# Four scalings of w_out moved from ScalarE to GpSimd, with a new hand-written order of steps

## The chip, the cores and the metric

The kernel runs on one core of a Trainium2 chip. The core has five engines that work side by side, each through its own queue in order: TensorE (PE in the profile; its weight loads are shown as PEld), VectorE (DVE), ScalarE (ACT), GpSimd (POOL) and SyncE (SP, which here only issues transfers). The metric is the device time of one execution in microseconds (us). Before the change it is 273.89 us, the median of three runs (273.89 to 274.06).

## What is computed

Two layers follow one another. The first is an attention without softmax, whose features are products of two small sketches; the second is a wide layer with a rational activation, applied to the first one's result.

```python
# attention: q, k, v are 4 batches x 4 heads x 1088 positions x 32; S1, S2 are 8 x 32
def phi(x):
    a = np.einsum('rd,bhsd->bhsr', S1, x)
    b = np.einsum('rd,bhsd->bhsr', S2, x)
    return np.einsum('bhsi,bhsj->bhsij', a, b).reshape(*x.shape[:-1], r * r)
q_p, k_p = (phi(q), phi(k))
kv = np.einsum('bhsf,bhsd->bhfd', k_p, v)
z = np.sum(k_p, axis=2)
num = np.einsum('bhsf,bhfd->bhsd', q_p, kv)
den = np.einsum('bhsf,bhf->bhs', q_p, z)[..., None] + 1e-06
x = num / den                        # then reshaped to 4352 tokens x 128
# wide layer: w_in is 128 x 2048, w_out is 2048 x 128
h = x @ w_in
P = a[0] + a[1] * h + a[2] * h2 + a[3] * h3
Q = 1.0 + np.abs(b[0]) * np.abs(h) + np.abs(b[1]) * h2
out = (P / (Q + 1e-06)) @ w_out
```

Here h2 and h3 are the square and the cube of h.

## The kernel before

**How the work is cut.** The tokens of the wide layer are cut into pieces, and with the 2048 hidden columns they make 17 units, numbered 0 to 16, of 128 x 4096 hidden values each. Unit 0 has the first 256 tokens and all its hidden columns, units 1 to 14 have 512 tokens and half the columns, units 15 and 16 have 256 tokens again. A unit's hidden values are made in four parts of 1024 columns and worked on in two halves of 2048.

**A unit's steps.** `hidden` (step h, line 448) is the matmul of tokens with w_in into a pair of PSUM tiles; `evac` (e, line 454) is ScalarE's copy of it to bf16, named hh; `d_abs`, `d_w`, `d_y` (u, w, y; lines 477, 483, 488, VectorE) make the denominator; `a_ln` and `a_exp` (ln, ex; lines 539, 543, ScalarE) turn it into its reciprocal r; the linear factor p = a3 h + a2 (pa on ScalarE, line 534, or pd on VectorE, line 529; the table `P_ON_ACT` says which, for each half of a unit); `d_s`, `d_hs`, `d_g` (s, m, x; lines 547, 551, 562, VectorE) multiply hh, r and p. In the halves listed in `HORNER` the factors are taken in another order, with one more small step (v, line 557). `gather` (G, line 581) is the output matmul of r, s and g with three scaled copies of w_out, so that P is never formed: the copy for r is a0 w_out, the one for s is a1 w_out, and the one for g is w_out in bf16. `store` (st, line 590) transposes an output tile on VectorE and writes it.

**The scaled copies of w_out.** `fetch_w` (step lw, line 643) loads w_out in two halves of 512 KB into a buffer, `w_out_sb_f`, that shares two slots with the w tiles of the units. `w_part` (step wo, lines 610 to 618) makes the three bf16 copies, each in two halves of 128 x 1024: wo:0 and wo:1 times a0, wo:2 and wo:3 times a1, wo:4 and wo:5 plain. The table `W_ENG` gives the engine of each: four on ScalarE and two (wo:2 and wo:4) on VectorE.

**The attention.** `Keys` has the steps kt, ks, kc, kf, kp, kk: VectorE transposes k, TensorE makes the sketches, ScalarE copies one of them, VectorE multiplies them to features, TensorE multiplies these with v, and ScalarE keeps the sums (`kvz`). Batch 0 does this in three parts, so as to begin early. `Queries` has qt, qs, qc, qf, qp (the same for q, then the numerators and denominators), qd, qi, qx (denominator, reciprocal, quotient), qb (a transpose on TensorE) and qk (ScalarE's copy into `xT`, what `hidden` reads). Batch 0 has four blocks, 0 to 3; the later batches have three each. From block 3 on, the sketches go through DRAM to be spread over the partitions (`Spread`, lines 395 to 426).

**What sets the order.** Nothing is scheduled by a planner at run time. `ORDER`, lines 21 to 57, is a list of 726 steps written as name:number; the program issues them in that order, so each engine's queue holds its share of them in the same order, and semaphores make a step wait for what it reads and for the buffers that it reuses. A step that isn't ready holds up everything behind it on its engine. The steps lx, lk, lv, lq, lw are loads on SP's queue; tn issues idle matmuls (line 170), as many as `TURNS` says: tn:0 ten, tn:1 and tn:4 two each.

Of the kernel before, what the change touches and what calls it, by code (L numbers as in the profile page):

```python
# [20 lines left out]
ORDER = """
tn:4 tn:0 lw:1 kt0:0 lq:0 kt2:0 lw:0 kt3:0 lx:1 kt1:0 ks0:0 lk:1 qt:0 ks2:0 kc0:0 lx:0 kf0:0 ba:0 qt:1 tn:1 kc2:0 qs:0
kf2:0 kp0:0 qc:0 ks1:0 qf:0 kc1:0 kf1:0 qs:1 wo:1 qt:3 kp1:0 qc:1 kp2:0 qf:1 qt:2 qs:3 wo:4 kk:0 lq:1 lv:1 wo:2 qp:0
wo:0 qs:2 qd:0 wo:5 qi:0 qx:0 qc:2 qb:0 qf:2 qk:0 wo:3 qp:1 kt0:1 qc:3 h2:0 qd:1 qi:1 qx:1 qt:5 h3:0 e2:0 qt:4 kt1:1
qp:2 e3:0 h1:0 pa1:0 u1:0 w1:0 h0:0 y1:0 qd:2 e1:0 qi:2 qx:2 qs:4 e0:0 qb:1 qb:2 qt:6 ks1:1 qk:1 u0:0 qk:2 ln1:0 w0:0
ks0:1 y0:0 h1:1 lk:2 kc1:1 ex1:0 lq:2 kf1:1 h3:1 e1:1 s1:0 kc0:1 h0:1 e3:1 kf0:1 pa0:0 m1:0 h2:1 qf:3 e0:1 x1:0 qp:3
qc:4 e2:1 kt0:2 h0:2 ln0:0 u1:1 kt1:2 h1:2 w1:1 e0:2 ex0:0 y1:1 ks0:2 h2:2 e1:2 s0:0 qd:3 ln0:1 h3:2 qi:3 m0:0 e2:2
lk:3 qx:3 kp1:1 x0:0 e3:2 ex0:1 u1:2 qb:3 lv:2 G0:0 pd0:1 qk:3 w1:2 ln1:1 G1:0 G2:0 qf:4 G3:0 kc0:2 kk:1 y1:2 ex1:1
G4:0 G5:0 kf0:2 qp:4 ln0:2 s0:1 qs:5 G0:1 qd:4 qc:5 qi:4 ex0:2 qt:7 G1:1 qx:4 m0:1 qb:4 ks1:2 qk:4 s1:1 pa1:1 h2:3
s0:2 kc1:2 m1:1 h3:3 e2:3 kf1:2 h1:3 e3:3 st:0 x1:1 ln1:2 qs:7 x0:1 h0:3 e1:3 kt1:3 m0:2 h2:4 e0:3 pd1:2 pa0:2 u1:3  # L30
h3:4 qt:9 w1:3 e2:4 G2:1 ex1:2 x0:2 h0:4 qf:5 e3:4 kp1:2 s1:2 pa0:3 y1:3 h1:4 qc:7 e0:4 m1:2 ln0:3 qp:5 kt0:3 e1:4
G3:1 x1:2 ex0:3 G4:1 m0:3 G5:1 u1:4 ks0:3 qd:5 ln1:3 qi:5 G0:2 w1:4 G1:2 pa1:3 qx:5 G2:2 y1:4 lv:3 qb:5 G3:2 qk:5
ex1:3 h0:5 m1:3 v0:3 kk:2 ln0:4 h2:5 s1:3 e0:5 qs:6 G4:2 qf:7 ex0:4 h1:5 x0:3 qt:8 qc:6 e2:5 s0:4 e1:5 h3:5 pd0:4
pa1:4 m0:4 h1:6 v1:3 e3:5 x0:4 G5:2 ln1:4 u1:5 h3:6 st:2 e1:6 w1:5 qp:7 ex1:4 x1:3 h0:6 e3:6 y1:5 qd:7 pa0:5 lq:3 G0:3
G2:3 qi:7 s1:4 h2:6 e0:6 m0:5 ln0:5 m1:4 qs:8 G3:3 e2:6 qf:6 G5:3 x1:4 ex0:5 G0:4 u1:6 G1:4 qc:8 ln1:5 qp:6 v0:5 qx:7
w1:6 qb:7 qd:6 G2:4 pa0:6 qi:6 G3:4 qx:6 y1:6 qb:6 qk:7 G4:4 qk:6 ex1:5 h3:7 m0:6 pa1:5 G5:4 qt:10 s1:5 h1:7 e3:7 st:4
h2:7 e1:7 m1:5 ln0:6 x0:5 h0:7 e2:7 x1:5 qs:9 e0:7 h3:8 qf:8 ex0:6 u1:7 h1:8 v0:6 qc:9 ln1:6 w1:7 ks1:3 s0:6 e1:8 G0:5
y1:7 kc1:3 qp:8 ex1:6 h2:8 pd1:6 kc0:3 e3:8 s1:6 ln0:7 h0:8 kf0:3 e2:8 m1:6 G2:5 ex0:7 G3:5 x0:6 G4:5 kf1:3 qd:8 e0:8
qs:10 G5:5 ln1:7 qi:8 u1:8 kp1:3 qx:8 pa0:7 w1:8 qb:8 G0:6 qf:9 qk:8 y1:8 qc:10 h3:9 ex1:7 s0:7 h2:9 e3:9 s1:7 ln0:8
h0:9 m0:7 e2:9 x1:6 G2:6 e0:9 h1:10 x0:7 ex0:8 pd1:7 h1:9 m1:7 pa0:8 s0:8 G3:6 e1:9 u1:9 G0:7 qt:11 ln1:8 qp:9 qt:12  # L40
u0:9 m0:8 h3:10 e1:10 w1:9 qd:9 ex1:8 qf:10 h2:10 x0:8 e3:10 G4:6 x1:7 e2:10 h0:10 y1:9 kk:3 pa0:9 w0:9 qp:10 qi:9
y0:9 e0:10 G1:7 qx:9 qd:10 ln0:9 s1:8 qb:9 G5:6 qi:10 u1:10 G2:7 qk:9 ex0:9 G3:7 qx:10 m1:8 qb:10 G4:7 qk:10 ln1:9
pd1:8 h1:11 s0:9 w1:10 ex1:9 qs:11 h0:11 m0:9 e1:11 x1:8 G5:7 qc:11 e0:11 h3:11 y1:10 pa1:9 h2:11 s1:9 e3:11 ln0:10
x0:9 G0:8 h0:12 m1:9 e2:11 pd0:10 ex0:10 h1:12 u1:11 x1:9 G1:8 ln1:10 w1:11 G0:9 G2:8 e1:12 s0:10 G3:8 e0:12 y1:11
h2:12 ex1:10 G4:8 m0:10 ln0:11 G1:9 qf:11 G5:8 s1:10 ex0:11 h3:12 x0:10 pa1:10 m1:10 qs:12 G2:9 s0:11 G3:9 e2:12 G4:9
pd0:11 qc:12 ln1:11 m0:11 qp:11 x1:10 G5:9 e3:12 x0:11 G0:10 qd:11 ex1:11 G1:10 qi:11 u1:12 G2:10 pa1:11 qx:11 G3:10
w1:12 qb:11 G4:10 s1:11 qk:11 pa0:12 h1:13 y1:12 h2:13 e1:13 m1:11 ln0:12 h3:13 st:6 x1:11 ex0:12 G5:10 qf:12 st:10
qp:12 e2:13 s0:12 e3:13 h0:13 st:8 ln1:12 m0:12 h2:14 u1:13 e0:13 x0:12 ex1:12 h3:14 u0:13 w1:13 e2:14 w0:13 G0:11
s1:12 e3:14 h1:14 pa1:12 y0:13 h0:14 m1:12 qd:12 e1:14 y1:13 G1:11 e0:14 qi:12 pd0:13 G2:11 ln1:13 qx:12 G3:11 u1:14
G4:11 ex1:13 x1:12 G5:11 w1:14 qb:12 G0:12 qk:12 ln0:13 G1:12 s1:13 h0:15 y1:14 ex0:13 h2:15 m1:13 e0:15 ln0:14 s0:13  # L50
h1:15 pd1:13 e2:15 m0:13 ex0:14 h3:15 x1:13 x0:13 e1:15 G2:12 e3:15 s0:14 G3:12 pa0:14 G4:12 u1:15 h2:16 m0:14 ln1:14
w1:15 G5:12 h3:16 x0:14 ex1:14 y1:15 G0:13 e2:16 G1:13 e3:16 s1:14 h0:16 ln0:15 st:12 u3:16 G2:13 u2:16 e0:16 w3:16
h1:16 w2:16 ex0:15 y3:16 pd0:15 G3:13 y2:16 e1:16 s0:15 G4:13 pa1:14 G5:13 u0:16 m0:15 G0:15 ln1:15 G1:15 w0:16 m1:14
G0:14 G1:14 ex1:15 y0:16 G2:14 pd1:15 G3:14 ln0:16 v1:14 x0:15 s1:15 ex0:16 G2:15 G3:15 x1:14 G4:15 ln2:16 m1:15 G0:16
ex2:16 s0:16 pa0:16 x1:15 G1:16 G5:14 s2:16 pa3:16 m0:16 G5:15 ln3:16 m2:16 x0:16 ex3:16 st:14 pa2:16 G2:16 s3:16
G3:16 st:15 G4:16 x2:16 m3:16 G5:16 G6:16 x3:16 G7:16 G8:16 st:16
""".split()
# [12 lines left out]
def kernel(  # L70
# [128 lines left out]
    for i in range(2):  # L199
        nc.vector.tensor_mul(out=S12[:, :, i, :],  # L200
                             in0=sT[i][:, None, 0:R].broadcast_to([128, H, R]),
# [408 lines left out]
    def w_part(x):  # L610
        y, f = x // 2, x % 2 * (nf // 2)
        o, t = w_sb[y][:, f:f + nf // 2], w_out_sb_f[:, f:f + nf // 2]
        if y == 2:
            (nc.scalar.copy if W_ENG[x] else nc.vector.tensor_copy)(out=o, in_=t)
        elif W_ENG[x]:
            nc.scalar.activation(out=o, in_=t, func=ACT.Copy, scale=a_sb[:, y:y + 1])
# [94 lines left out]
```

## Time and profile before

| | |
|---|---|
| median of three runs | 273.89 us (273.89 to 274.06) |
| the profiled execution | 274.08 us, of which its span, first to last instruction, 272.3 us |
| TensorE, busy | 258.4 us, 95% of the span |
| VectorE, busy | 256.0 us, 94% |
| ScalarE, busy | 250.2 us, 92% |
| GpSimd, busy | 2.9 us, 1%, all before 4.8 us |
| last VectorE instruction ends | 268.4 us; what follows is the last store |

Three engines are nearly full, so a share of the whole span does not tell them apart. The profile can be asked for a stretch of the span instead, for the instructions of a line, for a timeline of single instructions with the wait ahead of each in brackets, and for the waits of all engines added up. A line of the timeline gives the start, the length, the engine, the line of the kernel, the operation, and output <- inputs with their shapes; x12 at its end means that twelve in a row were drawn together.

### The profile page before, as it was taken

What the parts mean: (1) busy time and instruction counts of PE and PEld (TensorE: products, weight loads), DVE (VectorE), ACT (ScalarE), POOL (GpSimd) and SP (SyncE); (2) the same over time, 40 slices, a digit from 0 to 9 for tenths busy, and PEclk for the clock granted to TensorE, in tenths of its full rate; (3) what the DMA queues carried; (4) which work ended last, traced back from release to release, by engine and by line L of the source; (5) the groups of instructions that cost most, each with busy time, mean ns of one, the idle gap of its engine ahead of it and who ended that gap; (6) DMA issues with size and microseconds to landing.
All of it is one profiled execution on the core that took longest, in us unless ns stands there. A gap on an engine that the chain in (4) does not pass through costs nothing.

```text
span 272.3 us, 3730 instructions
## 1 busy us (share of the span) xinstructions
PE 258.4 (95%) x1398; PEld 146.2 (54%) x1398; DVE 256.0 (94%) x277; ACT 250.2 (92%) x224; POOL 2.9 (1%) x24
## 2 busy tenths in 40 slices
...
GB/s 166 290 330 99 196 14 183 101 50 100 2 80 135 12 136 81 67 78 39 96 6 115 12 0 4 40 90 0 14 97 90 25 0 0 2 24 14 1 7 74
DMA packets 30530, 19.55 MB, mean 72 GB/s; under 512 B 20400, under 2 KB 26672, under 8 KB 30512
## 3 DMA queue, kind: packets, MB, share of 16 engines
...
q8 instruction: 11, 0.18, 0.3%
...
## 4 chain that ended last, share of the span: by engine, by line
PE 35%; ACT 28%; DVE 23%; issue 9%; DMA 2%; SPq 1%; DVEq 0%; ACTq 0%
PE h_ps L448 17%; PE att_ps L581 9%; ACT hh L454 8%; ACT ln L539 7%; ACT r L543 7%; DVE s L547 4%; ACT p L534 4%; DVE g L551 4%; PE att_ps L361 3%; DVE g L562 3%; DVE w L488 3%; DVE w L483 2%; DMA k_sb<-in_k_dram 2%; PE att_ps L298 1%; PE att_ps L257 1%
## 5 line engine op out<-in xcount | busy, mean ns | idle before, releaser
L448 PE MATMUL h_ps<-xT,w_in_sb 128*128 128x512 f32 (+1 forms) x320 | 126.2, 536 | 2.3 <-ACT hh L454 1.6
L448 PEld LDWEIGHTS h_ps<-xT,w_in_sb 128*128 128x128 f32 x320 | 58.3, 190 | 52.8 <-issue 35.0
L454 ACT CAST hh<-h_ps 128x1024 bf16<-128x1024 f32 x68 | 68.2, 1022 | 4.2 <-PE h_ps L448 3.7
L581 PEld LDWEIGHTS <-w_out 128*128 128x128 bf16 x460 | 44.6, 98 | 46.0 <-issue 15.1
L543 ACT ACTIVATE r<-ln 128x2048 bf16<-128x2048 f32 (+1 forms) x35 | 65.9, 1883 | 0.3
L539 ACT ACTIVATE ln<-w 128x2048 f32<-128x2048 bf16 (+1 forms) x35 | 65.9, 1882 | 0.3
L534 ACT ACTIVATE p<-hh,a_sb 128x2048 bf16<-128x2048 bf16 (+1 forms) x23 | 46.7, 2035 | 0.1
L547 DVE TENSOR_TENSOR s<-hh,r 128x2048 bf16<-128x2048 bf16 (+2 forms) x33 | 40.9, 1243 | 0.2
L488 DVE TENSOR_TENSOR w<-w,u 128x4096 bf16<-128x4096 bf16 (+2 forms) x22 | 39.5, 1798 | 0.1
L581 PE MATMUL att_ps<-g,w_out 128*128 128x512 bf16 (+1 forms) x160 | 34.8, 347 | 3.6 <-DVE g L562 3.6
L551 DVE TENSOR_TENSOR g<-hh,s 128x2048 bf16<-128x2048 bf16 (+1 forms) x30 | 35.2, 1175 | 0.0
L581 PE MATMUL att_ps<-r,w_out 128*128 128x512 bf16 (+1 forms) x160 | 35.0, 347 | 0.0
L562 DVE TENSOR_TENSOR g<-g,p 128x2048 bf16<-128x2048 bf16 (+1 forms) x30 | 34.9, 1175 | 0.0
L581 PE MATMUL att_ps<-s,w_out 128*128 128x512 bf16 (+1 forms) x140 | 29.8, 343 | 0.9 <-DVE s L547 0.9
L483 DVE TENSOR_SCALAR w<-u,b_abs 128x4096 bf16<-128x4096 bf16 (+2 forms) x22 | 23.9, 1092 | 0.1
L477 DVE TENSOR_SCALAR u<-hh 128x4096 uint16<-128x4096 uint16 (+2 forms) x22 | 21.2, 968 | 0.9 <-ACT hh L454 0.8
L361 PEld LDWEIGHTS att_ps<-kvz,q_pT 128*128 128x128 f32 x144 | 17.6, 191 | 4.9 <-ACT sk_sb L408 1.0
L361 PE MATMUL att_ps<-kvz,q_pT 128*128 128x66 f32 x144 | 18.0, 274 | 0.9 <-DVE q_pT L353 0.5
L298 PEld LDWEIGHTS att_ps<-v_sb,k_p 128*64 128x64 f32 (+1 forms) x288 | 8.8, 138 | 2.6 <-issue 1.8
L529 DVE TENSOR_SCALAR p<-hh,a_sb 128x2048 bf16<-128x2048 bf16 x12 | 9.6, 799 | 0.0
L298 PE MATMUL att_ps<-v_sb,k_p 128*64 128x64 f32 (+1 forms) x288 | 9.5, 224 | 0.0
L425 DVE TENSOR_TENSOR q_pT<-a_all,b_all 128x768 f32<-128x768 f32 (+1 forms) x10 | 9.0, 896 | 0.0
...
## 6 DMA issues: line engine op xcount, KB each, us to landing
...
```

Source lines behind the costliest of these rows:

```text
L361: nc.tensor.matmul(self.nd[:, o:o + 2 * KW], lhsT=self.q_p[:, c, x:x + 128], rhs=kvz[self.b % 2][:, c, :], start=True, stop=True)
L448: nc.tensor.matmul(t[:, x * tl:(x + 1) * tl], lhsT=w_in_sb[:, f * 128:(f + 1) * 128], rhs=xT[:, t0:t0 + tl], start=True, stop=True)
L454: nc.scalar.copy(out=live[i]["hh"][:, part * PW:(part + 1) * PW], in_=live[i]["h", part])
L483: nc.vector.tensor_scalar(out=t[:, c], in0=live[i]["u"][:, c], scalar1=ab1, scalar2=ab0, op0=AX.mult, op1=AX.add)
L488: nc.vector.tensor_mul(out=t[:, c], in0=t[:, c], in1=live[i]["u"][:, c])
L534: nc.scalar.activation(out=part_of(i, "p", h), in_=hh, func=ACT.Identity, scale=a3, bias=a2)
L539: nc.scalar.activation(out=t, in_=live[i]["w"][:, span(h)], func=ACT.Ln, bias=1.0 + 1e-6)
L543: nc.scalar.activation(out=part_of(i, "r", h), in_=live[i]["ln"], func=ACT.Exp, scale=-1.0)
L547: nc.vector.tensor_mul(out=part_of(i, "s", h), in0=hh, in1=part_of(i, "r", h))
L551: nc.vector.tensor_mul(out=part_of(i, "g", h), in0=hh, in1=part_of(i, "p" if horner(i, first(h)) else "s", h))
L562: nc.vector.tensor_mul(out=g, in0=g, in1=part_of(i, "s" if horner(i, first(h)) else "p", h))
L581: nc.tensor.matmul(outs[t0][:, :tl], lhsT=w_sb[y][:, f0 + x, :], rhs=part_of(i, key, h)[:, c:c + tl], start=done[0] == 0, stop=done[0] == ...
```

## The change

`W_ENG` names GpSimd (2) for the four parts that ScalarE made, `w_part` learns that value, and `ORDER` is a new arrangement of the same 726 steps. `P_ON_ACT` and `HORNER`, which settle the engine and the form of each linear factor, are as they were, and so are `TURNS` and the lists of wide steps.

```diff
-W_ENG = (1, 1, 0, 1, 0, 1)
+W_ENG = (2, 2, 0, 2, 0, 2)
 P_ON_ACT = (1, 1, 0, 1, 1, 0, 1, 1, 0, 1, 1, 1, 1, 0, 1, 0, 1, 0, 1, 1, 0, 1, 0, 1, 1, 1, 0, 0, 1, 1, 0, 0, 1, 1)
...
         y, f = x // 2, x % 2 * (nf // 2)
         o, t = w_sb[y][:, f:f + nf // 2], w_out_sb_f[:, f:f + nf // 2]
         if y == 2:
-            (nc.scalar.copy if W_ENG[x] else nc.vector.tensor_copy)(out=o, in_=t)
+            (nc.vector.tensor_copy, nc.scalar.copy, nc.gpsimd.tensor_copy)[W_ENG[x]](out=o, in_=t)
+        elif W_ENG[x] == 2:
+            nc.gpsimd.tensor_scalar(out=o, in0=t, scalar1=a_sb[:, y:y + 1], scalar2=None, op0=AX.mult)
         elif W_ENG[x]:
             nc.scalar.activation(out=o, in_=t, func=ACT.Copy, scale=a_sb[:, y:y + 1])
```

The beginning of `ORDER`, up to the first steps on the second half of unit 0:

```diff
-tn:4 tn:0 lw:1 kt0:0 lq:0 kt2:0 lw:0 kt3:0 lx:1 kt1:0 ks0:0 lk:1 qt:0 ks2:0 kc0:0 lx:0 kf0:0 ba:0 qt:1 tn:1 kc2:0 qs:0
-kf2:0 kp0:0 qc:0 ks1:0 qf:0 kc1:0 kf1:0 qs:1 wo:1 qt:3 kp1:0 qc:1 kp2:0 qf:1 qt:2 qs:3 wo:4 kk:0 lq:1 lv:1 wo:2 qp:0
-wo:0 qs:2 qd:0 wo:5 qi:0 qx:0 qc:2 qb:0 qf:2 qk:0 wo:3 qp:1 kt0:1 qc:3 h2:0 qd:1 qi:1 qx:1 qt:5 h3:0 e2:0 qt:4 kt1:1
-qp:2 e3:0 h1:0 pa1:0 u1:0 w1:0 h0:0 y1:0 qd:2 e1:0 qi:2 qx:2 qs:4 e0:0 qb:1 qb:2 qt:6 ks1:1 qk:1 u0:0 qk:2 ln1:0 w0:0
...
+tn:0 lq:0 kt0:0 lx:1 kt2:0 lx:0 ks0:0 lw:0 kt3:0 kt1:0 ks2:0 kc0:0 lk:1 kf0:0 lw:1 qt:1 ks1:0 kc2:0 ba:0 tn:1 kf2:0
+kc1:0 tn:4 kp0:0 qt:0 qs:0 kf1:0 kp1:0 qt:2 qc:0 kp2:0 qf:0 qs:2 kk:0 lv:1 qc:2 qp:0 qs:1 qd:0 qf:2 qt:3 qp:2 wo:0
+qc:1 qi:0 lq:1 qx:0 qf:1 qs:3 qd:2 qb:0 qi:2 wo:4 qp:1 qk:0 qc:3 h3:0 qd:1 qi:1 qx:1 wo:2 wo:3 qx:2 h2:0 e3:0 kt0:1
+wo:1 kt1:1 h0:0 e2:0 wo:5 pa1:0 u1:0 h1:0 w1:0 y1:0 e0:0 ks1:1 qt:5 e1:0 qt:4 qb:2 qb:1 qs:4 qk:2 u0:0 qk:1 ln1:0 h1:1
+qt:6 w0:0 y0:0 kc1:1 ex1:0 h3:1 kf1:1 lk:2 ks0:1 e1:1 s1:0 lq:2 kc0:1 h0:1 e3:1 kf0:1 pa0:0 m1:0 h2:1 qf:3 x1:0 qc:4
...
```

In both kernels qd is a VectorE instruction for blocks 0 and 1 and a ScalarE instruction for all others.

More of the change, by code (lines that the diff above doesn't have):

```diff
@@ L21 @@
 ORDER = """
-tn:4 tn:0 lw:1 kt0:0 lq:0 kt2:0 lw:0 kt3:0 lx:1 kt1:0 ks0:0 lk:1 qt:0 ks2:0 kc0:0 lx:0 kf0:0 ba:0 qt:1 tn:1 kc2:0 qs:0
-kf2:0 kp0:0 qc:0 ks1:0 qf:0 kc1:0 kf1:0 qs:1 wo:1 qt:3 kp1:0 qc:1 kp2:0 qf:1 qt:2 qs:3 wo:4 kk:0 lq:1 lv:1 wo:2 qp:0
-wo:0 qs:2 qd:0 wo:5 qi:0 qx:0 qc:2 qb:0 qf:2 qk:0 wo:3 qp:1 kt0:1 qc:3 h2:0 qd:1 qi:1 qx:1 qt:5 h3:0 e2:0 qt:4 kt1:1
-qp:2 e3:0 h1:0 pa1:0 u1:0 w1:0 h0:0 y1:0 qd:2 e1:0 qi:2 qx:2 qs:4 e0:0 qb:1 qb:2 qt:6 ks1:1 qk:1 u0:0 qk:2 ln1:0 w0:0
-ks0:1 y0:0 h1:1 lk:2 kc1:1 ex1:0 lq:2 kf1:1 h3:1 e1:1 s1:0 kc0:1 h0:1 e3:1 kf0:1 pa0:0 m1:0 h2:1 qf:3 e0:1 x1:0 qp:3
@@ L27 @@
[L27 to L56, printed above, removed]
+tn:0 lq:0 kt0:0 lx:1 kt2:0 lx:0 ks0:0 lw:0 kt3:0 kt1:0 ks2:0 kc0:0 lk:1 kf0:0 lw:1 qt:1 ks1:0 kc2:0 ba:0 tn:1 kf2:0
@@ new lines @@
+kc1:0 tn:4 kp0:0 qt:0 qs:0 kf1:0 kp1:0 qt:2 qc:0 kp2:0 qf:0 qs:2 kk:0 lv:1 qc:2 qp:0 qs:1 qd:0 qf:2 qt:3 qp:2 wo:0
+qc:1 qi:0 lq:1 qx:0 qf:1 qs:3 qd:2 qb:0 qi:2 wo:4 qp:1 qk:0 qc:3 h3:0 qd:1 qi:1 qx:1 wo:2 wo:3 qx:2 h2:0 e3:0 kt0:1
+wo:1 kt1:1 h0:0 e2:0 wo:5 pa1:0 u1:0 h1:0 w1:0 y1:0 e0:0 ks1:1 qt:5 e1:0 qt:4 qb:2 qb:1 qs:4 qk:2 u0:0 qk:1 ln1:0 h1:1
+qt:6 w0:0 y0:0 kc1:1 ex1:0 h3:1 kf1:1 lk:2 ks0:1 e1:1 s1:0 lq:2 kc0:1 h0:1 e3:1 kf0:1 pa0:0 m1:0 h2:1 qf:3 x1:0 qc:4
+e0:1 qp:3 e2:1 kt0:2 h0:2 ln0:0 u1:1 h1:2 w1:1 qd:3 e0:2 ex0:0 kt1:2 y1:1 ks0:2 h2:2 e1:2 s0:0 ln1:1 h3:2 qi:3 m0:0
@@ new lines @@
+e2:2 kp1:1 qx:3 e3:2 x0:0 ex1:1 u1:2 qb:3 lv:2 G0:0 w1:2 qk:3 ln0:1 G1:0 y1:2 lk:3 G2:0 G3:0 kc0:2 ex0:1 qs:5 qf:4
+G4:0 kk:1 kf0:2 qc:5 qp:4 pa1:1 s0:1 G5:0 qt:7 qd:4 ln0:2 G0:1 qi:4 pd0:1 G1:1 qx:4 s1:1 qb:4 qs:7 qk:4 ex0:2 m0:1
+h3:3 m1:1 ln1:2 h2:3 s0:2 x0:1 ks1:2 e3:3 m0:2 e2:3 h0:3 kc1:2 pa0:2 st:0 kf1:2 h1:3 x1:1 e0:3 qs:6 e1:3 x0:2 h3:4
+ex1:2 u1:3 h0:4 pd1:2 e3:4 w1:3 pa0:3 h2:4 qf:5 y1:3 qp:5 qc:7 e0:4 e2:4 h1:4 s1:2 ln0:3 qt:9 kp1:2 m1:2 e1:4 kt0:3
+qd:5 ex0:3 x1:2 G2:1 G3:1 kt1:3 pa1:3 u1:4 G4:1 qi:5 G5:1 w1:4 lv:3 ln1:3 G0:2 qx:5 G1:2 qt:8 y1:4 lq:3 ex1:3 qb:5
@@ new lines @@
+G2:2 G3:2 qk:5 m1:3 G4:2 ln0:4 G5:2 qf:7 h1:5 s1:3 kk:2 qc:6 ex0:4 h0:5 m0:3 e1:5 ln1:4 v1:3 h2:5 s0:4 e0:5 v0:3 qp:7
+pd0:4 e2:5 m0:4 h3:5 ex1:4 x1:3 h3:6 qd:7 e3:5 x0:4 pa1:4 u1:5 h1:6 s1:4 e3:6 ks0:3 w1:5 e1:6 h0:6 pa0:5 st:2 x0:3
+h2:6 y1:5 e0:6 qs:8 e2:6 G0:3 m1:4 ln0:5 G2:3 G3:3 qf:6 qi:7 G5:3 m0:5 qc:8 ex0:5 qp:6 x1:4 G0:4 u1:6 qd:6 ln1:5 G1:4
+qi:6 w1:6 G2:4 pa0:6 G3:4 qx:7 qx:6 qb:7 y1:6 qb:6 qk:7 G4:4 qk:6 ex1:5 h1:7 m0:6 ln0:6 h3:7 s1:5 G5:4 e1:7 v0:5 e3:7
+h2:7 v0:6 kc0:3 pa1:5 m1:5 h0:7 qt:11 qf:8 e2:7 x1:5 qp:8 e0:7 kf0:3 ex0:6 qs:9 h3:8 u1:7 qc:9 ln1:6 x0:5 h1:8 w1:7
@@ new lines @@
+ex1:6 ks1:3 s0:6 G0:5 y1:7 kc1:3 e1:8 G2:5 qd:8 e3:8 G3:5 kf1:3 G4:5 ln1:7 h0:8 pd1:6 ex1:7 s1:6 h2:8 x0:6 e0:8 qi:8
+G5:5 m1:6 e2:8 G0:6 qx:8 ln0:7 u1:8 qb:8 kp1:3 qt:10 qk:8 w1:8 pa0:7 h2:9 qf:9 y1:8 ex0:7 qs:10 h3:9 qc:10 e2:9 x1:6
+ln0:8 qp:9 st:4 s0:7 h0:9 e3:9 pd1:7 ex0:8 m0:7 h1:9 s1:7 e0:9 x0:7 G2:6 kk:3 qd:9 e1:9 G3:6 s0:8 pa0:8 h1:10 u0:9
+m1:7 ln1:8 h3:10 u1:9 w0:9 e1:10 m0:8 G0:7 e3:10 G4:6 w1:9 ex1:8 h2:10 x0:8 y1:9 pa0:9 h0:10 y0:9 qi:9 G5:6 qf:10
+e0:10 x1:7 qp:10 ln0:9 qt:12 G1:7 qx:9 s1:8 qd:10 e2:10 qb:9 G2:7 qk:9 qi:10 u1:10 ex0:9 G3:7 G4:7 qx:10 m1:8 ln1:9
```

14 lines of the change are left out of this document (added).

## The prediction

> **What bounds the kernel now.** I read the busy times by stage first, because the page's single share (VectorE 94%, ScalarE 92%, TensorE 95%) averages over a start, a long middle and an end. The columns are the stretch, its length, then busy us and instructions of PE, PEld, DVE, ACT and POOL, the clock, and DMA share and GB/s.
>
> ```profile
> 6.00:28.00 22.00, 20.56 (x190) 16.59 (x189) 16.73 (x34) 14.12 (x25) 0.00 (x0) 1.00 0.84 241
> 28.00:266.50 238.50, 231.63 (x1190) 127.02 (x1190) 237.23 (x237) 234.78 (x199) 0.00 (x0) 1.00 0.22 54
> 266.50:272.30 5.80, 1.37 (x13) 0.96 (x10) 1.14 (x2) 0.00 (x0) 0.00 (x0) 0.95 0.45 66
> ```
>
> From 28.0 to 266.5 us VectorE is busy 237.23 of 238.50: it stands still 1.27 us in all. So in the middle the end is set by how much VectorE work is left at 28 us. Before that it is idle 5.3 of 22 us and TensorE is the fullest. The waits that remain are short (total us, times, longest):
>
> ```profile
> DVE qT L321 <- DMA q_sb<-in_q_dram: 2.1, 1, 2.1
> DVE out_sb L590 <- PE att_ps L581: 1.0, 2, 0.7
> DVE u L477 <- ACT hh L454: 0.8, 3, 0.3
> ```
>
> Only the first is large, and it lies in the start. There I read the timeline (start, length, engine, line, operation):
>
> ```profile
> 11.50 1.15 ACT L616 ACTIVATE w_out<-w_out_sb_f,a_sb 128x1024 bf16<-128x1024 f32 x1
> ...
> 14.93 1.15 ACT L616 ACTIVATE w_out<-w_out_sb_f,a_sb 128x1024 bf16<-128x1024 f32 x1
> ...
> 15.98 1.03 ACT L614 CAST w_out<-w_out_sb_f 128x1024 bf16<-128x1024 f32 x1
> ...
> 17.87 1.17 ACT L616 ACTIVATE w_out<-w_out_sb_f,a_sb 128x1024 bf16<-128x1024 f32 x1
> ...
> 17.96 1.11 PE L361 MATMUL att_ps<-kvz,q_pT 128*128 128x66 f32 x8 [0.52 <-DVE q_pT L353]
> ...
> 18.90 3.67 PE L448 MATMUL h_ps<-xT,w_in_sb 128*128 128x256 f32 x16
> ...
> 20.88 1.01 ACT L454 CAST hh<-h_ps 128x1024 bf16<-128x1024 f32 x1 [1.66 <-PE h_ps L448]
> ...
> 23.65 0.69 DVE L477 TENSOR_SCALAR u<-hh 128x2048 uint16<-128x2048 uint16 x1 [0.23 <-ACT hh L454]
> ...
> 27.44 0.51 DVE L321 STREAM_TRANSPOSE qT<-q_sb 128x320 f32<-128x320 f32 x1 [0.34 <-PE att_ps L402]
> ...
> 28.00 0.69 DVE L477 TENSOR_SCALAR u<-hh 128x2048 uint16<-128x2048 uint16 x1
> ```
>
> The four scalings to be moved sit in ScalarE's gaps. Each copy behind one began about when TensorE had finished its input (the copy at 12.64 against matmuls over at 12.6, the one at 17.07 against 17.04). After the first hidden matmuls ScalarE is again waiting, 1.66 us before 20.88. So the 1.15 + 1.15 + 1.03 + 1.17 = 4.5 us bought nothing but idle time.
>
> **The change, part by part.**
>
> *ScalarE loses four instructions, 4.5 us.* Gain on the path: 0 to 0.1 us, taken as 0, since they lay beside TensorE's start.
>
> *GpSimd gains four, 128x1024 each.* The trace has no such operation. Nearest rows:
>
> ```profile
> L212 POOL TENSOR_TENSOR SAB<-sT,mask 128x128 f32<-128x128 f32 x2 | 0.8, 398 | 0.0
> L184 POOL MEMSET kvz<- 128x132 f32 x2 | 0.4, 215 | 0.0
> L206 POOL COPY S<-S 128x32 f32<-128x32 f32 x2 | 0.4, 210 | 1.0 <-DVE S L200 1.0
> ```
>
> A memset of one column takes 0.10 us and of 132 columns 0.215, so 0.88 ns a column and 1.0 us for 1024: the low end. The copy's 0.11 us above 0.10 for 32 columns gives 3.4 ns and 3.6 us: the high end. A line through the copy and the two-input product (1.96 ns a column, 0.147 us fixed) gives 2.15 us, which I take: the copy is the same kind of work and the product the longest row. The w_out loads move from first and third among the six big loads behind v of batch 0 to fourth and sixth; at 512 KB and the 330 to 415 GB/s that the trace shows from 10 to 18 us, I put their landing at about 14.1 and 16.7. GpSimd then works from 14.1 to 23 (to 28.5 at the high end). The first reader is the output matmul at 48.6, and VectorE's w of unit 1, which reuses the buffer of the raw w_out and now waits for GpSimd, ran at 40.05; behind it on VectorE stand y and so ScalarE's ln. At least 11 us are to spare, so this costs nothing.
>
> *The linear factors.* Their table and the Horner list are unchanged in the diff: 23 instructions on ScalarE and 12 on VectorE in both orders. The 726 steps are the same set, so VectorE's and TensorE's work is unchanged in amount. Only positions move.
>
> *The start in the new order.* I replay it by hand with the start-to-start times of the rows above. Unchanged up to 8.9: key transposes, sketches. The third key sketch and four idle matmuls (0.22 us each) follow directly; the first key products run at 9.9 to 10.5. The first query sketch now waits for its transpose, queued behind the 1.4 us key product on VectorE (8.92 to 10.35): 10.75. From there TensorE is full: sketch 1.06, key products 1.68, sketch 1.11, numerators 1.04, sketch 1.06, numerators 0.94 (block 2, which before came between the hidden halves), 0.44 + 0.41 for the fourth block's sketch and a transpose back, numerators 0.94. The sum is 8.68, so the first hidden matmuls start at 19.4 (now 18.90). In return all 32 of unit 0 run in a row: 19.4 to 26.4 (now 26.85). ScalarE's second copy of hh ends at 24.1, its linear factor (2.0) and two more copies at 28.0. So u of the first half starts at 28.0, exactly as now, but one step that was done by then, the transpose at 27.44 (0.45 us), comes after it. Everything else ahead of u is the same set of steps. **Price: +0.45 us** of VectorE work carried into the full stage, with bounds 0.4 lower to 0.5 higher from my replay of the first hidden matmul.
>
> *The loads on SP.* q of batch 1 now stands behind v of batch 1, which waits for the last key products (13.5). All these bytes were in by 22 us; the transposes that read q now stand behind y, at 26.8, so the 2.13 us wait for q disappears. It covered time in which VectorE would have waited for hh until 23.65 anyway: gain 0. If q were later than 26.8, each us would push u one for one.
>
> *The middle and the end.* Summing the median spacing of each form, VectorE's steps from u at 28.0 would end at 266.87; they ended at 268.41. Of that 1.54 us, 0.87 is the wait for the last matmuls. The new order can win the other 0.67 or lose as much again; I take 0.
>
> *VectorE beside GpSimd.* VectorE's own two w_out steps (0.65 and 0.74 us, at about 18.6 and 20.4) fall among GpSimd's. VectorE has about 1.25 us of slack before its first u at 24.1. No row shows both engines at work, so the bounds are 0 and 2 us. I take 0.2.
>
> **Sum.** The profiled execution took 274.08 us (span 272.3). 274.08 + 0.45 + 0.2 = 274.73; the median of the runs is 0.19 lower, 273.89, so I forecast **274.5**. Differences under 0.2%, 0.55 us, are what a measurement of this kernel can't tell from none: faster means below 273.34, slower above 274.44.
>
> **The rivals.**
> 1. *Even, 273.9, chance 0.26.* The first hidden matmuls start at 18.9 as now, u at 27.55, and the leftover transpose fits in. For it: TensorE lost 0.52 us at 17.96 to a wait that the new order lacks. Against it: the extra numerators ahead of it.
> 2. *Faster, 272.9, chance 0.18.* VectorE's small waits in the middle are what the new order removes: the 0.67 us above, and 0.3 for dependent neighbours (15 now, 11 after, at some 0.07 each), with rival 1's start: 273.89 - 0.97. It decides once it exceeds the 0.45 by 0.55. For it: the order is new from end to end. Against it: 1.27 us of idle is all there is.
> 3. *GpSimd holds VectorE up, 275.8, chance 0.16.* If a VectorE step can't start while a GpSimd instruction runs, the two w_out steps and u lose half of 2.15 each, 3.2 us, less 1.25 of slack and some overlap: 1.5 on top of 274.34. For it: four GpSimd steps back to back up to 23. The Trainium skill (SBUF — State Buffer, "SBUF: two separate sides") says that GpSimd and VectorE share a pair of ports, held for a whole instruction, and that the loser waits. No run yet shows it here.
> 4. *Cold TensorE, 275.7, chance 0.10.* The rows:
>
> ```profile
> 1.19 4.89 PE L170 MATMUL att_ps<-idle 128*128 128x512 bf16 x12 [1.19 <-DVE idle L165]
> 8.39 0.59 PE L170 MATMUL att_ps<-idle 128*128 128x512 bf16 x2
> ```
>
> The first twelve come 0.43 us apart, the later two 0.22: the array runs at half speed until about 5.6. Now ten come first, over at 5.45, then a pause until the first key transpose at 6.4. If full speed isn't granted by then, the 14 sketch matmuls (0.11 each) take twice as long and the key product starts 1.2 later. The Trainium skill (TensorE: Matmul & The Clock Gate, Part 1) asks for one busy window of about 3.4 us, free-running; ten matmuls cover that only for some phases of the window.
>
> My forecast, 274.2 to 275.1, has 0.30. Slower: 0.16 + 0.10 + 0.28 of the forecast's; even takes 0.24 of rival 1 and 0.02 of the forecast; faster 0.18 and 0.02 of rival 1. The range 273.0 to 276.6 leaves out half of rival 2 and the far ends of 3 and 4.
>
> **What would show it.** Right: hidden matmuls from about 19.4, u of the first half near 28.0 with the transpose behind it, VectorE idle under 2 us from there, the w_out rows on POOL near 2 us ended by 23. Wrong: first u much before 23.5, or the end earlier though u is not; VectorE's w_out rows far longer than 0.65 and 0.74 (rival 3); idle matmuls or sketches 0.2 apart after 6.5 (rival 4).

## The result and the profile after

The changed kernel takes **276.31 us** in the median (275.02 to 278.76, 11 runs) against 273.90 (273.75 to 274.94, 11 runs) for the kernel before: a ratio of 1.0091, with a 95% interval of 1.0076 to 1.0107. It is slower by 2.4 us, inside the forecast range of 273.0 to 276.6 and 1.8 us above the predicted 274.5. Its runs also spread over 3.7 us where those of the kernel before lie within 1.2. The profiled execution took 277.25 us, with a span of 275.5.

First the middle row of the same table as before, for the kernel after (stretch, its length, busy us and instructions of PE, PEld, DVE, ACT, POOL, clock, DMA share, GB/s), and two narrow stretches around its beginning:

```profile
28.00:266.50 238.50, 231.17 (x1163) 125.48 (x1164) 236.04 (x236) 232.61 (x197) 0.00 (x0) 0.99 0.22 54
...
26.30:29.70 3.40, 1.43 (x13) 1.19 (x12) 3.37 (x4) 2.76 (x5) 1.53 (x2) 1.00 0.86 243
29.70:33.10 3.40, 3.19 (x7) 1.47 (x8) 2.93 (x5) 3.14 (x3) 0.00 (x0) 0.50 0.55 148
```

From 28 us to 266.5 VectorE is idle 2.46 us, 1.19 more than the 1.27 before. The narrow rows show where: TensorE is busy only 1.43 us of 26.3 to 29.7, and in the 3.4 us that follow its clock is 0.50. From 28 to 50 us alone VectorE is busy 20.52 us, where it was busy 21.75 before, so all of the added idle time lies there.

The timeline of that place, in the kernel after (start, length, engine, line, operation; in brackets the wait ahead of it):

```profile
16.05 2.85 POOL L616 TENSOR_SCALAR w_out<-w_out_sb_f,a_sb 128x1024 bf16<-128x1024 f32 x1 [11.31 <-DMA w_out_sb_f<-in_moe_w_out_dram]
...
19.10 7.12 PE L448 MATMUL h_ps<-xT,w_in_sb 128*128 128x256 f32 x32
...
20.50 5.89 POOL L616 TENSOR_SCALAR w_out<-w_out_sb_f,a_sb 128x1024 bf16<-128x1024 f32 x2 [1.61 <-DMA w_out_sb_f<-in_moe_w_out_dram]
...
23.85 1.36 DVE L477 TENSOR_SCALAR u<-hh 128x2048 uint16<-128x2048 uint16 x1 [1.38 <-ACT hh L454]
25.25 1.69 DVE L483 TENSOR_SCALAR w<-u,b_abs 128x2048 bf16<-128x2048 bf16 x1
26.35 1.48 POOL L614 CAST w_out<-w_out_sb_f 128x1024 bf16<-128x1024 f32 x1
26.98 1.94 DVE L488 TENSOR_TENSOR w<-w,u 128x2048 bf16<-128x2048 bf16 x1
28.83 1.02 DVE L321 STREAM_TRANSPOSE qT<-q_sb 128x384 f32<-128x384 f32 x2
29.91 0.91 PE L402 MATMUL att_ps<-qT,S 128*64 128x192 f32 x4 [2.18 <-DVE qT L321]
```

GpSimd's second w_out half lands only at 20.5, so GpSimd works until 27.83, straight across u, w and y of unit 0's first half. These three took 0.69, 0.81 and 1.23 us before; here they take 1.36, 1.69 and 1.94, together 2.26 us more. The transposes behind them (steps qt:5 and qt:4) come that much later, TensorE stands 2.18 us waiting for them, and then its clock is halved: the eight hidden matmuls at 30.82 take 4.79 us where the same eight take 3.70 at full speed in the kernel a_warm below. The second half's u starts at 29.79 (28.00 before). In this one execution the account is 1.79 us from u's later start, 0.45 for the transpose that now lies behind it, and 1.19 of idle time: 3.4, against a span that is 3.2 longer. Which part of this the median pays is a question for the experiments; each is a kernel with a short name, given where its time stands (a_ for an edit of the kernel after, b_ for one of the kernel before).

### The profile page after: what moved, and what is told of

Same layout as the page of the kernel before. It is cut to its first block, busy times and chain, and to the rows that moved or that the text cites. A ratio compares the mean times of both kernels' runs of the same rounds, so it can differ in the third digit from the quotient of the medians.

```text
span 275.5 us, 3744 instructions
## 1 busy us (share of the span) xinstructions
PE 260.7 (95%) x1398; PEld 147.5 (54%) x1398; DVE 258.4 (94%) x277; ACT 246.4 (89%) x220; POOL 13.1 (5%) x28
## 4 chain that ended last, share of the span: by engine, by line
PE 37%; DVE 30%; ACT 17%; issue 10%; DMA 4%; SPq 0%; DVEq 0%; ACTq 0%
PE h_ps L448 17%; PE att_ps L581 9%; DVE g L551 7%; DVE s L547 6%; ACT hh L454 5%; ACT r L543 5%; DVE g L562 4%; ACT ln L539 4%; PE att_ps L361 4%; DVE w L488 3%; DVE w L483 3%; ACT p L534 3%; PE att_ps L298 3%; DVE u L477 2%; DMA k_sb<-in_k_dram 2%
## 5 line engine op out<-in xcount | busy, mean ns | idle before, releaser
L448 PEld LDWEIGHTS h_ps<-xT,w_in_sb 128*128 128x128 f32 x320 | 59.1, 191 | 52.7 <-issue 37.7
L454 ACT CAST hh<-h_ps 128x1024 bf16<-128x1024 f32 x68 | 67.4, 1021 | 4.5 <-PE h_ps L448 4.4
L488 DVE TENSOR_TENSOR w<-w,u 128x4096 bf16<-128x4096 bf16 (+2 forms) x22 | 40.2, 1829 | 0.1
L483 DVE TENSOR_SCALAR w<-u,b_abs 128x4096 bf16<-128x4096 bf16 (+2 forms) x22 | 24.9, 1132 | 0.2
L477 DVE TENSOR_SCALAR u<-hh 128x4096 uint16<-128x4096 uint16 (+2 forms) x22 | 22.0, 1002 | 1.7 <-ACT hh L454 1.6
L616 POOL TENSOR_SCALAR w_out<-w_out_sb_f,a_sb 128x1024 bf16<-128x1024 f32 x3 | 8.7, 2920 | 12.9 <-DMA w_out_sb_f<-in_moe_w_out_dram 12.9
```

The lines of the kernel that those rows point to most:

```text
L448: nc.tensor.matmul(t[:, x * tl:(x + 1) * tl], lhsT=w_in_sb[:, f * 128:(f + 1) * 128], rhs=xT[:, t0:t0 + tl], start=True, stop=True)
L454: nc.scalar.copy(out=live[i]["hh"][:, part * PW:(part + 1) * PW], in_=live[i]["h", part])
L483: nc.vector.tensor_scalar(out=t[:, c], in0=live[i]["u"][:, c], scalar1=ab1, scalar2=ab0, op0=AX.mult, op1=AX.add)
L488: nc.vector.tensor_mul(out=t[:, c], in0=t[:, c], in1=live[i]["u"][:, c])
```

## The experiments

Ratios are to the kernel before, run on the same chip in the same rounds (its medians lay between 273.90 and 273.96); the brackets after a ratio are its 95% interval. They are not ratios of the medians: where the runs of a kernel stand in groups, the ratio lies nearer that of the means.

**The four scalings left out, in both kernels.** In each, VectorE sets those four parts of w_out to zero before 6 us, and the steps issue nothing:

```diff
         elif name == "wo":
-            w_part(i)
+            if W_ENG[i] != OUT:
+                w_part(i)
```

> The old order with the four scalings of ScalarE left out (zeros as in the run beside it; the output isn't the reference's). If the 4.5 us lay in ScalarE's gaps, the time stays within 0.3 us of 273.9. If they stood on the path of the start, it falls by 0.5 us or more; then taking them from ScalarE is worth something that the change gave back elsewhere.

Measured (b_noscale): 273.87 us (273.71 to 274.85), ratio 1.0004 [0.9995, 1.0012]. The 4.5 us on ScalarE were worth nothing, as forecast: they lay in gaps.

> The new order with the four scalings left out: those parts of w_out are zeros, set by VectorE in its idle time before 6 us, so the output isn't the reference's. If GpSimd's work holds VectorE up (theory 1), u, w and y of unit 0 come back from 1.36, 1.69 and 1.94 us to about 0.69, 0.81 and 1.23, TensorE's pause at 27.7 goes, the clock stays full, and the time is before plus the 0.45 us of the leftover transpose: 274.3, between 273.9 and 274.7. If the new order itself is slow (theory 2), the time stays above 275.3.

Measured (a_noscale): 274.63 us (273.43 to 276.29), 1.0036 [1.0017, 1.0054]. Without GpSimd's work u, w and y are back at 0.70, 0.81 and 1.23 us, and the time falls by 1.7 us. But it does not fall to the kernel before, and the runs stand in three groups: 273.43 and 273.82 with a mean granted clock of 1.0; seven from 274.55 to 274.96 at 0.990 to 0.994; three from 276.05 to 276.29, two of them at 0.987 and one at 0.998. A second cause is left, and it does not strike every run. The profiled execution shows one, in three consecutive stretches of this kernel (columns as above):

```profile
4.91:8.32 3.41, 2.06 (x15) 1.50 (x13) 3.00 (x8) 0.21 (x1) 0.00 (x0) 1.00 1.06 257
8.32:11.74 3.42, 3.42 (x18) 2.03 (x18) 2.13 (x3) 0.61 (x3) 0.00 (x0) 0.50 1.00 285
11.74:15.15 3.41, 3.41 (x82) 2.90 (x80) 1.83 (x3) 0.70 (x3) 0.00 (x0) 1.00 1.01 336
```

TensorE is granted half its clock from 8.32 to 11.74, after a stretch in which it was busy only 2.06 us. The first hidden matmul starts at 20.72; in the profile of the kernel after, whose clock held at the start, it was 19.10. One such stretch lowers the mean clock over 275 us by 0.006 (half of 3.4 us), which is how far most runs of the kernel after lie below 1.0: six of its eleven are at 0.993 or 0.994 (275.6 to 278.1 us), one at 0.985 (278.76), and four from 0.997 to 0.999, of which three took 275.0 to 275.2 and one 276.75. No profile of the kernel after shows this fall at the start, though: in its one profiled execution, at 0.994, the clock held at the start and fell behind the pause. A lower mean clock alone does not tell the two places apart.

**The idle matmuls at the start, one edit in each kernel.** In the kernel before the two idle matmuls of tn:4 are taken from the front and put where the change has them; in the kernel after they are put back in front. Everything else stays.

```diff
-tn:4 tn:0 lw:1 kt0:0 ... ba:0 qt:1 tn:1 kc2:0
+tn:0 lw:1 kt0:0 ... ba:0 qt:1 tn:1 tn:4 kc2:0
```

> The kernel before with one step moved: tn:4 behind tn:1, so that ten idle matmuls come first and four later. If ten are too few, the time rises from 273.9 by 0.5 to 1.5 us, its runs spread into groups 0.7 to 2 us apart, and the granted clock falls to about 0.990 in some. If the start of the old order is dense enough without them, it stays at 273.9 within 0.2.

Measured (b_ten): 276.55 us (274.18 to 277.8), 1.0078 [1.0049, 1.0108]: two matmuls of no use moved by some 8 us cost 2.63 us in the median, 2.1 in the mean. TensorE's timeline in this kernel:

```profile
6.47 2.78 PE L257 MATMUL h_ps<-S,kT 128*128 128x64 f32 x14 [1.49 <-DVE kT L251]
9.05 1.91 PE L170 MATMUL att_ps<-idle 128*128 128x512 bf16 x4
...
22.22 3.67 PE L448 MATMUL h_ps<-xT,w_in_sb 128*128 128x256 f32 x16
```

The ten idle matmuls end at 4.98, TensorE then waits 1.49 us for the first transposed keys, its clock is halved from 7.59 to 14.42 (the four idle matmuls at 9.05 take 1.91 us; four take 1.03 in the kernel after, whose clock held), and the first hidden matmul starts at 22.22 instead of 18.90. Again it depends on the run: four of the twelve took 274.2 to 274.4 at a clock of 0.998 to 0.999, two 275.7 to 276.0 at 0.993 to 0.994, and six more than 277. Three of these six show a mean clock of 1.0, which this reading does not explain; only one of the six was profiled.

> The changed kernel with one step moved back: tn:4, two idle matmuls, ahead of tn:0 as in the old order, so that twelve and not ten come first. The runs of the changed kernel so far fall into groups, and their traces show the clock halved for one or two stretches of 3.41 us either near 8 us or after the pause at 27.7. If ten idle matmuls are too few for the start (theory: clock at the start), the half-speed stretches near 8 us go and the time falls to about 275.1, with what is left being GpSimd's hold on VectorE and the pause. If the start plays no part, it stays at 276.3 within 0.4.

Measured (a_tn): 274.68 us (274.1 to 275.56), 1.0026 [1.0015, 1.0037], all ten runs at 0.996 or more. **Two idle matmuls back in front take away 1.63 us of the 2.4, and most of the spread.** The low clocks are gone at the pause too, so the 1.63 us need not all be the start's. In the profiled execution GpSimd works from 20.52 to 28.16, over u, w and y as in the kernel after, but only u is longer (1.32 us); w and y have their old lengths, and one of GpSimd's scalings took 3.39 us instead. So which of the two engines loses is not the same in each execution. The pause ahead of the sketch is 0.55 us here, not 2.18, and the second half's u starts at 28.14:

```profile
23.84 1.32 DVE L477 TENSOR_SCALAR u<-hh 128x2048 uint16<-128x2048 uint16 x1 [1.42 <-ACT hh L454]
...
28.14 0.65 DVE L477 TENSOR_SCALAR u<-hh 128x2048 uint16<-128x2048 uint16 x1
```

**The pause behind y.** In the first edit the transposes qt:5 and qt:4 go ahead of the stretched u; in the second nine idle matmuls fill TensorE's pause; the third joins the first one with a_tn.

```diff
-wo:1 kt1:1 h0:0 e2:0 wo:5 pa1:0 u1:0 h1:0 w1:0 y1:0 e0:0 ks1:1 qt:5 e1:0 qt:4 qb:2 qb:1 qs:4
+wo:1 kt1:1 h0:0 e2:0 wo:5 pa1:0 qt:5 qt:4 u1:0 h1:0 w1:0 y1:0 e0:0 ks1:1 e1:0 qb:2 qb:1 qs:4
...
-TURNS = (10, 2, 0, 0, 2, 0, 0, 0, 0)
+TURNS = (10, 2, 0, 0, 2, 9, 0, 0, 0)
...
-qb:2 qb:1 qs:4
+qb:2 qb:1 tn:5 qs:4
```

> The changed kernel, with the two transposes of q of batch 1 put ahead of u of unit 0 again, as the old order has them. VectorE stays stretched by GpSimd (u, w, y about 2.2 us longer in all), but TensorE's fourth-block sketch no longer waits behind them. If the larger part of the loss is TensorE's pause and the half-speed clock after it, the time falls to about 275.0, the clock reads 0.999 and the runs spread by less than 0.5 us. If the stretched VectorE alone makes the loss, the time stays within 0.4 us of 276.3.

Measured (a_qt_early): 275.16 us (273.91 to 276.92), 1.0048 [1.0027, 1.0069]. The time is near what was expected, but the reason given was not the whole one: clocks go down to 0.986 and the spread is 3 us. The start's clock is untouched, and in the profiled execution (276.03 us) it falls from 7.63 to 14.46:

```profile
4.22:7.63 3.41, 2.33 (x16) 1.58 (x15) 2.12 (x6) 0.81 (x2) 0.51 (x2) 1.00 1.06 267
7.63:11.04 3.41, 3.41 (x16) 2.02 (x17) 2.20 (x4) 0.61 (x3) 0.00 (x0) 0.50 1.05 335
```

Three runs at 0.999 and 1.0 took 273.91 to 274.37, but three more at 0.997 and 0.998 took 275.64 to 276.25. As with three runs of b_ten, the mean clock does not explain these.

> The changed kernel, with nine idle matmuls (0.22 us each) issued ahead of the sketch that waits at 27.7 us, so that TensorE is busy through the pause. The pause itself stays. If the half-speed stretch is a cost of its own, the clock reads 0.999, the first matmuls after the pause take 0.6 us and not 1.2, the time falls by 0.5 to 1.5 us to about 275.3 and the spread from 275.0 to 278.8 shrinks to under 0.5 us. If it costs nothing, because VectorE is behind anyway, the time stays at 276.3 within 0.4.

Measured (a_warm): 275.93 us (275.1 to 278.13, 6 runs), 1.0094 [1.0058, 1.0129]. In the profiled execution (275.31 us) the idle matmuls run from 27.87 to 29.76, the clock holds, and the eight hidden matmuls after them take 3.70 us instead of 4.79:

```profile
30.16 3.70 PE L448 MATMUL h_ps<-xT,w_in_sb 128*128 128x512 f32 x8
```

In these two profiles the clock falls with the pause and holds without it. The median moved by 0.4 us, less than the spread, and the ratio is no better than the 1.0091 of the kernel after; a gain was not shown. One of the six runs took 278.12 us at a mean clock of 1.0.

> Both: the two transposes of q ahead of u, and twelve idle matmuls first; GpSimd still makes the four scalings. If GpSimd's hold costs only through the pause of TensorE and through the clock, this comes to 274.0 within 0.3, the runs within 0.6 us of one another, level with before. If the stretched u, w and y cost in themselves, it stays at 274.8 or above.

Measured (a_fix): 274.74 us (273.65 to 277.0; that longest run at a clock of 0.992, the others at 0.996 or more), 1.0029 [1.001, 1.0048]. The 274.0 of the first case was not reached: with twelve idle matmuls in front, taking the pause away as well gained nothing over a_tn's 274.68. The profile has w at 1.68 and y at 1.93 us, 1.57 more than unstretched, with no such pause behind them. The second half's u starts at 29.07, against 28.40 in the version without GpSimd's work that follows (a_act_tn), and the last product before the end at 267.34 against 266.62: 0.67 us late at 28 us is 0.72 late at the end. What is left in this profile is lost by VectorE ahead of the second u, not by what TensorE does after it. But not all of it is lengthening. The transposes put ahead of u waited for the load of q:

```profile
23.86 1.04 DVE L321 STREAM_TRANSPOSE qT<-q_sb 128x384 f32<-128x384 f32 x2 [1.14 <-DMA q_sb<-in_q_dram]
24.82 0.65 DVE L477 TENSOR_SCALAR u<-hh 128x2048 uint16<-128x2048 uint16 x1
```

ScalarE's second copy of hh had ended at 24.10, so u starts about 0.7 us later than it could have: the edit brought in a price of its own, and a_fix is no clean measure of the stretch.

**The new order without GpSimd, and GpSimd in the new order but earlier.** `W_ENG` goes back to ScalarE in the first, tn:4 to the front, w_out's loads to the places they had, and the ScalarE scalings next to its query copies. The second is the same with GpSimd named again.

```diff
-tn:0 lq:0 kt0:0 lx:1 kt2:0 lx:0 ks0:0 lw:0 kt3:0 kt1:0 ks2:0 kc0:0 lk:1 kf0:0 lw:1 qt:1
+tn:4 tn:0 lw:1 lq:0 lw:0 lx:1 kt0:0 kt2:0 ks0:0 kt3:0 kt1:0 ks2:0 kc0:0 lk:1 lx:0 kf0:0 qt:1
...
+qc:0 wo:1 ... qc:2 wo:3 ... qc:3 wo:5 wo:0
...
-W_ENG = (2, 2, 0, 2, 0, 2)
+W_ENG = (1, 1, 0, 1, 0, 1)
```

> The new order with the four scalings on ScalarE again, placed in its gaps (behind the copies of blocks 0, 2 and 3), the loads of w_out where the old order has them, and twelve idle matmuls first. The run without scalings came to 273.4 and 273.8 where its clock was full. If the new order is sound and GpSimd and the clock made the loss, this gives 273.6 within 0.3. If the new order is slower by itself (the 0.45 us of the leftover transpose), 274.3.

Measured (a_act_tn): **273.70 us** (273.37 to 274.3), 0.9991 [0.9983, 1.0000], the lowest median of this study. VectorE's timeline and its middle:

```profile
28.40 0.69 DVE L477 TENSOR_SCALAR u<-hh 128x2048 uint16<-128x2048 uint16 x1 [0.19 <-ACT hh L454]
29.01 0.51 DVE L321 STREAM_TRANSPOSE qT<-q_sb 128x320 f32<-128x320 f32 x1
```

```profile
28.00:266.50 238.50, 231.78 (x1187) 127.23 (x1185) 237.59 (x239) 235.16 (x200) 0.00 (x0) 1.00 0.23 56
```

The transpose does lie behind u, and u is 0.4 us later than before. That is the +0.45 of the forecast, and more: with u 0.40 later, 0.85 us of VectorE's steps have moved to behind 28.0. Yet the last product runs at 266.62, where it was 266.53, and the median is 0.2 us shorter. From 28 to 266.5 VectorE is idle 0.91 us where it was 1.27, so 0.36 was won by shorter waits; the other 0.4 would be closer spacing of neighbouring steps, which these rows don't show.

This profile also bears on the clock. In the stretch with the pause behind the key sketches TensorE was busy 2.27 us, and the clock stayed full:

```profile
7.60:11.00 3.40, 2.27 (x31) 1.80 (x29) 2.67 (x4) 0.61 (x3) 0.00 (x0) 1.00 1.01 273
11.00:14.40 3.40, 3.40 (x75) 2.87 (x72) 1.71 (x3) 2.00 (x6) 0.00 (x0) 1.00 1.10 354
```

a_tn and a_act_tn can be compared here as well. In a_tn's profile the second u starts at 28.14, 0.26 us before the 28.40 of this one, although u was stretched; its first hidden matmul had started 0.62 us earlier (19.09 against 19.71). It still ends later, with the last product at 266.91. On the way VectorE waits 0.51 us ahead of 87.33 for a transfer of the sketches (into `b_all`), a wait that the profile of the kernel after has too, ahead of 90.32, and this one has not.

> The kernel of a_act_tn (new order, twelve idle matmuls first, w_out loaded early) with the four scalings on GpSimd and nothing else changed. GpSimd can begin at about 11 us and end near 21, ahead of u of unit 0 at 24. If only its overlap with u, w and y costs (theory: GpSimd holds VectorE's steps on SBUF), this is level with a_act_tn, 273.7 within 0.3, and u, w and y take 0.69, 0.81 and 1.23. If GpSimd costs wherever it runs, 274.4 or more.

Measured (a_pool_early): 273.94 us (273.59 to 274.37), 0.9997 [0.9988, 1.0006]. With w_out loaded early GpSimd runs from 11.30 to 20.78, and u comes after it:

```profile
18.10 1.49 DVE L614 CAST w_out<-w_out_sb_f 128x1024 bf16<-128x1024 f32 x1
...
23.96 0.69 DVE L477 TENSOR_SCALAR u<-hh 128x2048 uint16<-128x2048 uint16 x1 [1.03 <-ACT hh L454]
```

VectorE's copy of w_out is stretched (0.64 us in a_act_tn), and so is its scaling at 20.29 (1.04 us against 0.74), but u then still waits 1.03 us for ScalarE, so the stretch is paid out of slack. **The same four instructions cost 0.24 us here (273.94 - 273.70), with intervals of the two ratios that overlap, while the two versions with late loads and twelve idle matmuls first lie 0.98 (a_tn) and 1.04 (a_fix) above the same 273.70.**

**GpSimd in the old order.** The old `ORDER` with the new `W_ENG` and `w_part`.

> The old order with the four scalings on GpSimd, no other change; twelve idle matmuls come first and the loads of w_out are early. GpSimd works from about 11.5 to 21.5. There VectorE's own two steps on w_out stand ahead of the denominator at 16.0. If GpSimd holds them, each for up to 2.9 us, the first hidden matmuls move from 18.9 to 19.5 or later and the time rises by 0.3 to 1.5 us. If it holds nothing there, the time stays at 273.9 within 0.2.

Measured (b_pool): 273.95 us (273.58 to 274.36), 1.0001 [0.9993, 1.001]. The second of the two cases came out. GpSimd worked from 11.29 to 21.29, and VectorE's scaling of w_out at 14.77 took 1.53 us (0.74 before), its copy just ahead 0.65 as before; the next step waits for TensorE's denominators and started at 16.22 (16.02 before); u started at 23.63, where it was 23.65. So the change of engine alone costs nothing in the old order.

**A stream of GpSimd work through the middle.** 41 scalings into scratch, one of 128x384 and forty of 128x512, issued after qk:5, beside VectorE's full stage:

```diff
             getattr(blocks[i](), q_does[name])()
+            if name == "qk" and i == 5:
+                nc.gpsimd.tensor_scalar(out=scrap[:, 0:384], in0=xT[:, 1472:1856], scalar1=a_sb[:, 0:1], scalar2=None, op0=AX.mult)
+                for _ in range(STREAM):
+                    nc.gpsimd.tensor_scalar(out=scrap, in0=w_in_sb[:, 0:512], scalar1=a_sb[:, 0:1], scalar2=None, op0=AX.mult)
```

> The kernel before with 41 more GpSimd scalings (f32 to bf16, 128x512, into a scratch tile that nobody reads) back to back from about 60 us on, in the full stage. One look, to measure the disputed cost by kind of VectorE step. If the two engines exclude each other on SBUF, VectorE's steps that read and write SBUF alone (u, w, p; s, m, x, y) take longer beside GpSimd, by half to all of their length, steps with a PSUM operand (x_tok, the key features, the output transpose) do not, and the GpSimd instructions lengthen too when VectorE is ahead; the run ends 10 to 40 us later. If the stretch in the changed kernel had another cause (transfers at 24 to 29 us), all VectorE steps keep their lengths.

Measured (b_stream): 286.5 us, one run, 12.5 more than the kernel before. VectorE's groups between 88 and 204 us, inside the stream (line, operation and shapes, count, then busy us and mean ns of one):

```profile
L564 DVE TENSOR_TENSOR g<-g,p 128x2048 bf16<-128x2048 bf16 x11 | 15.3, 1402 | 0.0
L479 DVE TENSOR_SCALAR u<-hh 128x4096 uint16<-128x4096 uint16 x6 | 8.3, 1378 | 0.1
L531 DVE TENSOR_SCALAR p<-hh,a_sb 128x2048 bf16<-128x2048 bf16 x5 | 5.8, 1152 | 0.0
L427 DVE TENSOR_TENSOR q_pT<-a_all,b_all 128x768 f32<-128x768 f32 x4 | 3.8, 951 | 0.0
L383 DVE TENSOR_TENSOR x_tok<-att_ps,rec 128x384 f32<-128x384 f32 x5 | 2.7, 548 | 0.1
```

Without the stream these five take 1211, 1210, 799, 950 and 545 ns in the kernel before. Most of the bf16 and uint16 steps lengthen (not all: the product of hh and p keeps its 1215 to 1221 ns, in the two that fall here); the f32 product of two SBUF tiles and the product that reads PSUM do not. Added up over all the VectorE groups that lengthened, (mean inside - mean without) x count comes to 12.0 us, nearly the whole 12.5.

## Why the forecast came out as it did

The time lies inside the range, and the direction was right, but by luck in part: the largest term of the sum, the leftover transpose, was worth nothing at the end, and the two mechanisms that made the kernel slower stood among the rivals, with 0.26 of chance between them. Their sizes were wrong too.

- **"ScalarE loses four instructions ... Gain on the path: 0": right.** b_noscale measures 1.0004.
- **The start's replay: right for the first half, wrong behind it.** Hidden matmuls from 19.10 in a row (19.4 predicted), first u at 23.85 (24.1). The second u came at 29.79, not 28.0, because of the next two points.
- **"GpSimd then works from 14.1 to 23": the step that failed first.** Both terms were too small. A scaling took 2.92 us in the mean, not 2.15 (the cast 1.48), and the halves of w_out landed at 16.05 and 20.5, not 14.1 and 16.7. The end was 27.83, close to the 28.5 that I had as the high end, and from that end I drew no consequence for VectorE: I costed GpSimd by its readers at 40 us and later, and looked for VectorE's steps beside it only up to 23.
- **"VectorE beside GpSimd ... I take 0.2": mis-sized.** It is 1.0 to 1.7, within the bounds of 0 and 2: a_tn less a_act_tn is 0.98, which takes in the late loads and whatever else differs between the two orders of the start, and the kernel after less a_noscale is 1.68, which takes in the pause and its clock. The two w_out steps named there hardly mattered: only the first stretched (0.65 to 1.45 us). What stood on the path was u, w and y, 2.26 us longer in the profiled execution, which the wrong end at 23 had left out. That is rival 3 by its mechanism but not by its form: VectorE's steps are slowed, not kept from starting. The Trainium skill (SBUF — State Buffer, "SBUF: two separate sides") says that the pair of ports which GpSimd shares with some kinds of VectorE instruction goes to whoever starts first for the whole instruction and that the other fully blocks. The trace doesn't agree: GpSimd's third scaling ran from 23.56 to 26.40, and u began and ended inside it, at 23.85 and 25.21.
- **Rival 4, cold TensorE, "price 1.2, chance 0.10": it struck, beside rival 3.** By a_tn the two idle matmuls are worth 1.63 us of the median, by a_noscale less a_act_tn 0.93, and by b_ten 2.63 us in the old order. The rows for it were in the prediction: twelve idle matmuls, then ten, and a pause before the keys arrive. I gave it one chance in ten on the ground of the profile of one execution. But whether the clock holds depends on the run, and a kernel whose lead-in only just suffices shows it as a spread, which one profile can't. The Trainium skill (TensorE: Matmul & The Clock Gate, Part 1) has the clock follow a free-running window of 3413 ns, and the half-speed stretches here, 3.4 and 6.8 us long, agree with that. It puts the fall of the clock after an idle window; here it fell after windows in which TensorE was busy 1.43, 1.86 (b_ten), 2.06 and 2.33 us (a_qt_early) of 3.41. It held after 2.92 in the kernel before, but also in a_act_tn, where TensorE was busy 2.27 us from 7.60 to 11.00. Since no fall shows where the clock's own stretches begin in a_act_tn, it stays open how little work lets the clock fall.
- **"+0.45" for the leftover transpose: in place, worth nothing at the end.** With the new order and the scalings on ScalarE, in a_act_tn, u is 0.4 us late with the transpose behind it, and the time is 0.9991 of the kernel before. "The middle ... I take 0" is the term that was off: the profile of a_act_tn has it win 0.76 us of the 0.85 back by the last product, close to the 0.67 that the prediction held possible and gave to rival 2.

The sum, remade from runs: -0.2 for the order with twelve idle matmuls first (a_act_tn), +0.98 for GpSimd with the late loads (a_tn over a_act_tn; of this 0.24, not clear of noise, is the engine by itself, a_pool_early, and 0.74 the late loads and the overlap that they bring), +1.63 for the two idle matmuls (a_tn to after) give +2.4. As each term is the difference of two neighbouring kernels, the sum must come out; the shares depend on the order in which the causes are taken. The other way round, the clock comes first with 0.93 (a_noscale over a_act_tn, which differ too in the place of w_out's loads and in ScalarE's scalings, worth nothing in b_noscale) and GpSimd's work last with 1.68 (after over a_noscale). So the two share some 0.7 us, in which the pause behind y with its half-speed window may stand, and which of them is the larger is not shown. Nor is it shown that the 0.98 is all stretch of u, w and y, since a_tn's profile has its second u early and its loss later on. A share of the pause alone could not be shown: a_fix removed it but waited for q, and a_warm's spread hides what it gained.
